# Packing k and v of eight heads so that scores and folds run as eight 64x32 products at a time

## The chip, the cores and the metric

The kernel runs on one core of a Trainium2 chip. The metric is the device time of one execution in microseconds. A core has five engines that run side by side, each through its own list of instructions in order: TensorE (PE in the profile; PEld are its weight loads), VectorE (DVE), ScalarE (ACT), GpSimd (POOL) and SyncE (SP, which here only issues DMAs). TensorE multiplies a stationary matrix, of up to 128 rows and 128 columns here, with a moving one and writes into PSUM, which this kernel uses as eight banks of 512 float32 values on each of 128 partitions. A product may use only some of the array's rows and columns: the profile writes `128*32` for one on all 128 rows and 32 of the columns.

## The reference

```python
def _attn_ref(q, k, v, phi):                 # (8 batches, 8 heads, 576, 64), phi (8, 8, 576, 32)
    a = np.exp(phi - np.max(phi, axis=2, keepdims=True))
    a = a / (np.sum(a, axis=2, keepdims=True) + 1e-09)
    k_m = np.einsum('bhsm,bhsd->bhmd', a, k)          # 32 memories per head
    v_m = np.einsum('bhsm,bhsd->bhmd', a, v)
    scores = (1.0 / np.sqrt(64)) * np.matmul(q, k_m.transpose(0, 1, 3, 2))
    attn = np.exp(scores - np.max(scores, axis=-1, keepdims=True))
    attn = attn / (np.sum(attn, axis=-1, keepdims=True) + 1e-09)
    return np.matmul(attn, v_m)

def _moe_ref(x, w_in, w_out):                # x: (4608, 512), w_in (512, 2048), w_out (2048, 512)
    h = x @ w_in
    return (h * np.cos(h)) @ w_out
```

The attention's output, with the heads side by side, is the x of the second function.

## The kernel before

The product attn · v_m · w_in is regrouped. For each batch `v_m` is multiplied into `w_in` first (the *fold*), which gives a matrix `vw` of 256 rows (8 heads x 32 memories) and 2048 columns, in four quarters `q` of 512 columns. The second layer's input is then attn times `vw`. The 4608 tokens run in 12 groups (`grp`) of 384, and each group in 16 steps `f` of 128 columns of h, 192 steps in all. One step is

- `gemm1` (L493): `hp = vw · aT`, six float16 products, two halves g of the rows times three pairs of high and low parts (12 products of 192 columns in a group that straddles two batches; float32 in group 0),
- `act` and `act_end`: h·cos h by ACT L502, DVE L507 and L508, ACT L512 (the sine), DVE L516 (which is the last to read `hp`), ACT L518 and DVE L519, giving `gp`,
- `gemm2` (L537), four steps behind `gemm1`: nine products that add into three banks `acc`.

The names in the views are those of these tiles: `hp_4_7` is step 7 of group 4, `gp_4_7` what it becomes, `acc_4_0` the first of its sums.

Beside the steps runs the preparation of the next batches, as a generator `prep(b)` that a table of jobs advances a little in each step. `memory(b)` exponentiates phi, multiplies it with k and v in one accumulation `psA` (L247, 40 products), divides by the sums (`X`, L261) and transposes that on TensorE (`tpx`). From `tpx` come `km` and `vm`. `attend(b)` then forms the scores in three blocks of 256, 256 and 64 tokens (L349), transposes each in squares of 32 from PSUM into SBUF on DVE (L351), takes the softmax there and transposes back into `aT`.

Heads lie in pairs: 64 partitions hold an even head's k, the other 64 an odd head's. So `km` is [128, 4 pairs, 64 columns], with the 32 columns of the one head zero on the partitions of the other, and one product of 128 rows and 64 columns makes the scores of two heads. GpSimd clears `km` and `vm` for that in each batch. `vm` is laid out the same way with the halves exchanged, and `fold_psum` uses it for the float32 folds of batch 0 (in `fold_first`, tiles `pvf`) and batch 1. For batches 2 to 7 `scales` splits `vm` into float16 parts: `vp`, the high part on all 128 rows for one head (it meets the high and the low part of `w_in` there), and `vl`, the low part, which has 64 rows of values and 64 of zeros. A fold of half g and quarter q is then four products with `vp` and four with `vl`, all of 128 rows and 32 columns, added in one bank `pv`. `split_fold` turns `pv` into the two float16 parts of `vw` (ACT L438, DVE L439).

PSUM is given out by three pools: `ps_acc` with three banks for `acc`, `ps_h` with three for `hp`, and `ps_s` with two for all small things: the memory products, `tpx`, scores and folds. The order on each engine is set by a scheduler in the framework, which takes the program's order, the pools and its own costs; a wait for a bank or a result holds up everything behind it on that engine.

## Time and profile before

| | |
|---|---|
| median of 3 runs | 718.53 us (717.75 to 719.26) |
| the profiled execution | 718.65 us, of which 716.6 us is the span that the profile shows |
| TensorE busy | 694.8 us, 97% of the span |
| VectorE, ScalarE busy | 570.0 us, 80%, and 520.8 us, 73% |
| GpSimd busy | 14.1 us, 2% |
| gemm2 (L537), gemm1 in float16 (L493) | 1584 and 1440 products |
| folds of batches 2 to 7 (L432) | 384 products |
| scores (L349) | 192 records for 96 products, since a float32 product is two |

Busy times are sums over instructions that may overlap: two products on different columns of the array each count in full. The time between the starts of successive groups in the timeline is the better measure of what something costs on TensorE. An idle engine costs nothing unless the engine at the bound waits for it. In rows by form, the columns are line, engine, operation, output and inputs, the part of the array used, the shape, and the count; then busy time and mean nanoseconds of one; then idle time before, and what ended it.

### The profile page before, as it was taken

The numbers are of one execution on the slowest core, as the hardware profiler recorded it, in microseconds if no ns is written. First come the engines' busy times: TensorE is split into PE (matmuls) and PEld (weight loads), VectorE is DVE, ScalarE is ACT, GpSimd is POOL, SyncE is SP. The second block draws the span as 40 slices with busy tenths as digits, with TensorE's granted clock in tenths as the row PEclk, the third lists the DMA queues.
The fourth block names the chain that finished last, engine by engine and source line by source line (L and its number), as shares of the span: only waits on it lengthen the run. The fifth ranks groups of instructions, "written<-read, shape, count | busy, mean of one in ns | idle before, by whom it ended". The sixth has DMA issues, their size and how long they took to land.

```text
span 716.6 us, 12018 instructions
## 1 busy us (share of the span) xinstructions
PE 694.8 (97%) x4578; PEld 357.2 (50%) x4578; DVE 570.0 (80%) x1256; ACT 520.8 (73%) x965; POOL 14.1 (2%) x34
## 2 busy tenths in 40 slices
PE   7689999999999999999999999999999999999997
PEld 3244444565454445565444544666444544555553
DVE  2868999998988997679877997679776987676753
ACT  1789999899886875668757685678767785665653
POOL 0000000000000000000000100000000000000000
PEclk9799999999999999999999999999999999999999
DMA  8995881426405300152103310152100000100101
GB/s 291 381 330 168 310 291 42 121 60 188 149 7 161 111 1 1 45 167 67 45 1 123 107 49 1 45 167 68 44 1 1 22 24 1 45 1 1 45 0 45
DMA packets 31561, 66.78 MB, mean 93 GB/s; under 512 B 2192, under 2 KB 11024, under 8 KB 31504
## 3 DMA queue, kind: packets, MB, share of 16 engines
q1 hardware_dynamic: 27184, 58.15, 25.1%
q10 hardware_dynamic: 4320, 7.87, 2.9%
q8 instruction: 36, 0.59, 0.3%
q14 instruction: 21, 0.17, 0.1%
HBM read 52.38 MB, written 9.44 MB: 86 GB/s over the span
## 4 chain that ended last, share of the span: by engine, by line
PE 60%; ACT 17%; DVE 16%; DMA 4%; issue 2%; SPq 1%; POOL 0%; ACTq 0%; DVEq 0%
PE acc L537 34%; PE hp L493 18%; PE pv L432 3%; ACT u L512 2%; DVE u L516 2%; DMA phi<-in_phi 2%; DVE u L508 2%; DVE gp L519 2%; ACT u L502 2%; ACT L512 2%; DVE gp L507 1%; DMA kv<-in_kv 1%; PE sc L349 1%; ACT L237 1%; PE psA L247 1%
## 5 line engine op out<-in xcount | busy, mean ns | idle before, releaser
L537 PE MATMUL acc<-wo,gp 128*128 128x512 f16 x1584 | 371.2, 379 | 0.0
L537 PEld LDWEIGHTS <-gp 128*128 128x128 f16 x1584 | 153.4, 98 | 161.5 <-issue 2.6
L493 PE MATMUL hp<-aT,vw 128*128 128x192 f16 (+1 forms) x1440 | 202.6, 284 | 0.8 <-DVE u L516 0.4
L493 PEld LDWEIGHTS <-vw 128*128 128x128 f16 x1440 | 125.1, 98 | 82.3 <-issue 30.0
L512 ACT ACTIVATE u<-u 128x384 f32<-128x384 f32 x192 | 99.7, 522 | 86.6 <-DVE u L508 85.7
L516 DVE SCALAR_TENSOR_TENSOR u<-hp,u 128x384 f32<-128x384 f32 x176 | 96.8, 552 | 45.7 <-ACT u L512 43.4
L502 ACT ACTIVATE u<-hp,cu 128x192 f32<-128x192 f32 (+1 forms) x240 | 110.3, 491 | 18.2 <-PE hp L493 11.8
L519 DVE TENSOR_TENSOR gp<-u,gp 128x384 f16<-128x384 f32 x176 | 96.6, 551 | 29.9 <-ACT gp L518 29.3
L518 ACT CAST gp<-u 128x384 f16<-128x384 f32 x176 | 89.0, 509 | 38.7 <-DVE u L516 36.7
L508 DVE TENSOR_TENSOR u<-u,gp 128x384 f32<-128x384 f32 x192 | 105.7, 552 | 3.2
L507 DVE CAST gp<-u 128x384 int32<-128x384 f32 x192 | 67.4, 353 | 20.6 <-ACT u L502 18.9
L532 PE MATMUL acc<-wo,gp 128*128 128x512 f32 x96 | 45.5, 603 | 1.6 <-DVE gp L514 1.6
L439 DVE SCALAR_TENSOR_TENSOR vw<-pv,vw 128x512 f16<-128x512 f32 x48 | 33.0, 689 | 5.1 <-ACT vw L438 3.8
L438 ACT ACTIVATE vw<-pv 128x512 f16<-128x512 f32 x48 | 28.3, 590 | 7.4 <-PE pv L432 6.5
L484 PE MATMUL hp<-aT,vf 128*128 128x384 f32 x64 | 26.4, 546 | 4.2 <-DVE gp L514 2.0
L512 ACT ACT_TABLE_LOAD x23 | 29.5, 1283 | 0.4
L532 PEld LDWEIGHTS acc<-wo,gp 128*128 128x128 f32 x96 | 17.0, 190 | 20.7 <-issue 14.9
L247 PE MATMUL psA<-kv,phi 128*32 128x129 f32 (+1 forms) x640 | 23.5, 276 | 2.8 <-DMA kv<-in_kv 1.5
L553 ACT ACTIVATE ob<-acc,os 128x512 f32<-128x512 f32 x28 | 18.5, 682 | 8.1 <-PE acc L537 5.2
L247 PEld LDWEIGHTS psA<-kv,phi 128*32 128x32 f32 (+1 forms) x640 | 16.1, 109 | 13.3 <-issue 6.9
L484 PEld LDWEIGHTS hp<-aT,vf 128*128 128x128 f32 x64 | 12.5, 207 | 17.7 <-DVE gp L514 4.6
L349 PE MATMUL sc<-q,km 128*64 128x256 f32 (+3 forms) x192 | 20.6, 343 | 0.0
(126 smaller groups left out, 549.5 us busy)
## 6 DMA issues: line engine op xcount, KB each, us to landing
kv<-in_kv SPq DMA_DIRECT2D x32, 516.0 KB, 5.8
q<-in_qT SPq DMA_DIRECT2D x8, 1152.0 KB, 6.4
raw_out<-in_w_out SPq DMA_DIRECT2D x8, 1024.0 KB, 5.0
out<-ob ACTq DMA_DIRECT2D x30, 256.0 KB, 2.1
raw_in<-in_w_in SPq DMA_DIRECT2D x6, 1024.0 KB, 8.4
phi<-in_phi SPq DMA_DIRECT2D x8, 512.0 KB, 7.2
w_in_sb<-w_in_parts SPq DMA_DIRECT2D x12, 256.0 KB, 4.1
phiT<-in_phiT SPq DMA_DIRECT2D x4, 576.0 KB, 6.4
```

Source lines behind the costliest of these rows:

```text
L247: nc.tensor.matmul(psA[32 * j:32 * (j + 1), g * KV:(g + 1) * KV], lhsT=a[:n, c, h * M:(h + 1) * M], rhs=kvs[c][:n, h * KV:(h + 1) * KV], s ...
L484: nc.tensor.matmul(hp[:, :GT], lhsT=st["vf", q][:, g, fo * P:(fo + 1) * P], rhs=st["aTf"][:, g], start=(g == 0), stop=(g == 1))
L493: nc.tensor.matmul(hp[:, c0:c0 + n], lhsT=vw[:, wi, g, fo * P:(fo + 1) * P], rhs=aT[:, ai, g, c1:c1 + n], start=(k == 0), stop=(k == 5))
L502: ins = nc.scalar.activation(u[:, c0:c0 + n], hp[:, c0:c0 + n], AF.Copy, scale=st["cu", b] if grp else 1.0 / (2.0 * math.pi), bias=0.25)
L507: nc.vector.tensor_copy(out=ni, in_=u)
L508: nc.vector.tensor_tensor(out=u, in0=u, in1=ni, op=ALU.subtract)
L512: nc.scalar.activation(u, u, AF.Sin, scale=TWO_PI_BELOW)
L516: nc.vector.scalar_tensor_tensor(out=u, in0=hp[:, :GT], scalar=2.0 ** -17, in1=u, op0=ALU.mult, op1=ALU.mult)
L518: nc.scalar.copy(gp[:, 0], u)
L519: nc.vector.tensor_tensor(out=gp[:, 1], in0=u, in1=gp[:, 0], op=ALU.subtract)
L532: nc.tensor.matmul(accs[grp][t], lhsT=gp[:, t * P:(t + 1) * P], rhs=wo[:, f + 1], start=(f == 0), stop=(f == NF - 1))
L537: nc.tensor.matmul(accs[grp][t], lhsT=gp[:, gi, t * P:(t + 1) * P], rhs=parts[:, wi], start=(f == 0 and gi == 0 and wi == 0), stop=(f == N ...
```

## The change

Heads 0 to 3 have k on the lower 64 partitions and heads 4 to 7 on the upper; v lies the other way round, and q and `w_in` are laid out on the host to match. So `km`, `vm` and `vl` have no zeros any more and are [128, 4, 32]: row half g belongs to heads 4g to 4g+3, and column j of four to the j-th of these. The clearing of `km` and `vm` on GpSimd, the mask for the maximum of v, and its multiplication on DVE go.

A product with `km`, with float32 `vm`, or with `vl` now uses 64 rows and 32 columns. `scores` and `fold_32` issue eight of them, alternating between the two row halves, and each half writes a bank of its own. A score block so takes two banks of `ps_s` and two transposes in place of one; a fold takes both halves g at once, in one step of four where it was two steps of two. In `fold_16` the first pass with `vp` stays as it was, four products of 128 rows for each g, and the second pass with `vl` is eight products of 64 rows. `fold_first` makes two copies of 256 columns in place of one of 512. To make room in `ps_s`, `psA` is taken from `ps_h`, gemm1's pool.

```diff
-    vl = const.tile([P, NP, 2, M], F16, name="vl")
-    nc.vector.memset(vl, 0.0)
+    vl = const.tile([P, NP, M], F16, name="vl")
...
-        psA = small_ps(f"psA_{b}")
+        psA = ps_h.tile([P, 512], F32, tag="ps_h", name=f"psA_{b}")
...
-        km = wk.tile([P, NP, 2 * M], F32, tag="km", name=f"km_{b}", bufs=1)
-        vm = wk.tile([P, NP, 2 * M], F32, tag="vm", name=f"vm_{b}")
-        nc.gpsimd.memset(km, 0.0)
-        nc.gpsimd.memset(vm, 0.0)
...
+        km = wk.tile([P, NP, M], F32, tag="km", name=f"km_{b}", bufs=1)
+        vm = wk.tile([P, NP, M], F32, tag="vm", name=f"vm_{b}")
+        tv = tpx[:, 0:HM].rearrange("p (g j m) -> p g j m", g=2, m=M)
+        for g in range(2):
+            nc.scalar.mul(km[HALF[g]], tv[HALF[g], g], 1.0 / math.sqrt(D))
+            nc.vector.tensor_copy(out=vm[HALF[1 - g]], in_=tv[HALF[1 - g], g])
...
-        nc.vector.tensor_tensor(out=l1, in0=l1, in1=vmask.rearrange("p g t -> p (g t)"), op=ALU.mult)
...
         def scores(i):
             t0, n = BL[i]
-            sc = small_ps(f"sc_{b}_{t0}")
+            sc = [small_ps(f"sc_{b}_{t0}_{g}") for g in range(2)]
+            for j in range(4):
+                for g in range(2):
+                    nc.tensor.matmul(sc[g][M * j:M * (j + 1), :n], lhsT=km[HALF[g], j], rhs=qt[HALF[g], j, t0:t0 + n],
+                                     start=True, stop=True)
             for g in range(2):
-                for p in range(2):
-                    nc.tensor.matmul(sc[D * p:D * (p + 1), g * n:(g + 1) * n], lhsT=km[:, 2 * g + p],
-                                     rhs=qt[:, 2 * g + p, t0:t0 + n], start=True, stop=True)
-            nc.vector.transpose(at[:, 2 * t0:2 * (t0 + n)], sc[:, :2 * n])
+                nc.vector.transpose(at[:, 2 * t0 + g * n:2 * t0 + (g + 1) * n], sc[g][:, :n])
...
+    def fold_32(b, pv, f):
+        for j in range(4):
+            for g in range(2):
+                v = HALF[1 - g]
+                nc.tensor.matmul(pv[g][M * j:M * (j + 1)], lhsT=st["vm", b][v, j], rhs=w_in_sb[v, j, f],
+                                 start=True, stop=True)
+
+    def fold_16(b, pv, q):
+        w2 = st["w2", q]
+        for g in range(2):
+            for j in range(4):
+                nc.tensor.matmul(pv[g][M * j:M * (j + 1)], lhsT=st["vp", b][:, j, 1 - g], rhs=w2[:, j, 1 - g],
+                                 start=True, stop=False, skip_group_check=True)
+        for j in range(4):
+            for g in range(2):
+                v = HALF[1 - g]
+                nc.tensor.matmul(pv[g][M * j:M * (j + 1)], lhsT=vl[v, j], rhs=w2[v, j, 1 - g],
+                                 start=False, stop=True, skip_group_check=True)
...
-    def fold(b, q, g):
-        if g == 0:
-            st["vw", b, q] = wk.tile([P, 2, 2, FS], F16, tag="vw", name=f"vw_{b}_{q}", bufs=8)
-        split_fold(b, st["vw", b, q], g, fold_psum(b, q, g))
+    def fold(b, q):
+        st["vw", b, q] = vw = wk.tile([P, 2, 2, FS], F16, tag="vw", name=f"vw_{b}_{q}", bufs=8)
+        pv = [small_ps(f"pv_{b}_{q}_{g}") for g in range(2)]
+        if b < 2:
+            fold_32(b, pv, slice(q * FS, (q + 1) * FS))
+        else:
+            fold_16(b, pv, q)
+        for g in range(2):
+            split_fold(b, vw, g, pv[g])
...
-            for g in range(2):
-                folds.setdefault(use - before + 4 * q + 2 * g, []).append((b, q, g))
+            folds.setdefault(use - before + 4 * q, []).append((b, q))
```

What this does to the order of instructions is shown at three places. In these rows each line gives the source line, the operation, output and inputs (with the buffers' numbers) and the shape of the output; line numbers behind the change are shifted by a few.

First, TensorE at the first quarter of batch 4's fold, before:

```order
L537 MATMUL acc_4_2_2937<-wo_85,gp_4_15_3439 128x512
L432 LDWEIGHTS vp_4_3590
L432 MATMUL pv_4_0_0_3598<-w_in_2_0_953,vp_4_3590 32x512
...
L432 LDWEIGHTS vl_86
L432 MATMUL pv_4_0_0_3598<-w_in_2_0_953,vl_86 32x512
...
L493 LDWEIGHTS vw_3_1_2711
```

and after:

```order
L538 MATMUL acc_4_2_3065<-wo_79,gp_4_15_3571 128x512
L427 LDWEIGHTS vp_4_3722
L427 MATMUL pv_4_0_0_3730<-w_in_2_0_1032,vp_4_3722 32x512
...
L427 MATMUL pv_4_0_1_3731<-w_in_2_0_1032,vp_4_3722 32x512
...
L432 LDWEIGHTS vl_80
L432 MATMUL pv_4_0_0_3730<-w_in_2_0_1032,vl_80 32x512
...
L432 MATMUL pv_4_0_1_3731<-w_in_2_0_1032,vl_80 32x512
...
L494 LDWEIGHTS vw_3_1_2828
```

Before, four products with `vp` and four with `vl` stand together for g = 0, and those for g = 1 (pv_4_0_1) two steps later. After, four and four with `vp` for both g are followed by eight with `vl`, which alternate between the two banks.

Second, the scores of batch 5. TensorE before:

```order
L537 MATMUL acc_5_2_3627<-wo_85,gp_5_14_3956 128x512
L349 MATMUL sc_5_0_4156<-q_5_3382,km_5_4073 64x256 x4
L349 MATMUL sc_5_256_4162<-q_5_3382,km_5_4073 64x256 x4
L493 LDWEIGHTS vw_4_0_3597
L493 MATMUL hp_6_3_4168<-aT_4_3259,vw_4_0_3597 128x384
...
L537 MATMUL acc_5_0_3625<-wo_85,gp_5_15_3989 128x512
...
L349 MATMUL sc_5_512_4207<-q_5_3382,km_5_4073 64x64 x4
```

and after:

```order
L538 MATMUL acc_5_2_3770<-wo_79,gp_5_14_4088 128x512
L343 MATMUL sc_5_0_0_4285<-q_5_3514,km_5_4216 32x256
L343 MATMUL sc_5_0_1_4286<-q_5_3514,km_5_4216 32x256
...
L494 LDWEIGHTS vw_4_0_3729
L494 MATMUL hp_6_3_4309<-aT_4_3373,vw_4_0_3729 128x384
...
L343 MATMUL sc_5_256_0_4297<-q_5_3514,km_5_4216 32x256
L343 MATMUL sc_5_256_1_4298<-q_5_3514,km_5_4216 32x256
...
L538 MATMUL acc_5_2_3770<-wo_79,gp_5_15_4121 128x512
...
L343 MATMUL sc_5_512_0_4348<-q_5_3514,km_5_4216 32x64
```

The two blocks of 256 stood next to each other, each in one of the two banks; now each takes both banks, and four products of gemm1 stand between them. On VectorE the same place reads before:

```order
L516 SCALAR_TENSOR_TENSOR u_6_2_4134<-hp_6_2_4127,u_6_2_4134 128x384
L351 STREAM_TRANSPOSE at_5_4153<-sc_5_0_4156 128x512
L519 TENSOR_TENSOR gp_6_2_4135<-u_6_2_4134,gp_6_2_4135 128x384
L351 STREAM_TRANSPOSE at_5_4153<-sc_5_256_4162 128x512
L355 TENSOR_REDUCE rm_5_4154<-at_5_4153 128x16
```

and after:

```order
L517 SCALAR_TENSOR_TENSOR u_6_2_4263<-hp_6_2_4256,u_6_2_4263 128x384
L346 STREAM_TRANSPOSE at_5_4282<-sc_5_0_0_4285 128x256
L346 STREAM_TRANSPOSE at_5_4282<-sc_5_0_1_4286 128x256
L520 TENSOR_TENSOR gp_6_2_4264<-u_6_2_4263,gp_6_2_4264 128x384
L350 TENSOR_REDUCE rm_5_4283<-at_5_4282 128x16
L346 STREAM_TRANSPOSE at_5_4282<-sc_5_256_0_4297 128x256
L346 STREAM_TRANSPOSE at_5_4282<-sc_5_256_1_4298 128x256
```

Each transpose became two of half the size, and the first pair stands ahead of the work that the second block's transposes follow.

Third, TensorE at the memory products of batch 4, with gemm1 of group 4. Before:

```order
L493 MATMUL hp_4_6_3007<-aT_3_2234,vw_3_1_2711 128x192
L537 LDWEIGHTS gp_4_2_2837
...
L493 MATMUL hp_4_7_3059<-aT_3_2234,vw_3_1_2711 128x192
...
L247 MATMUL psA_4_2958<-kv_4_0_2136,phi_4_2133 32x129 x8
L247 MATMUL psA_4_2958<-kv_4_1_2138,phi_4_2133 32x129 x8
...
L537 MATMUL acc_4_2_2937<-wo_85,gp_4_3_2899 128x512
L247 MATMUL psA_4_2958<-kv_4_3_2142,phi_4_2133 32x129 x8
...
L493 MATMUL hp_4_8_3107<-aT_2_1681,vw_2_2_2315 128x192
```

and after:

```order
L538 MATMUL acc_4_2_3065<-wo_79,gp_4_3_3027 128x512
...
L538 MATMUL acc_4_0_3063<-wo_79,gp_4_4_3054 128x512
L245 MATMUL psA_4_3075<-kv_4_0_2249,phi_4_2246 32x129 x8
L494 LDWEIGHTS vw_2_1_2223
L494 MATMUL hp_4_5_3084<-aT_2_1765,vw_2_1_2223 128x192
...
L245 MATMUL psA_4_3075<-kv_4_1_2251,phi_4_2246 32x129 x8
...
L494 MATMUL hp_4_6_3124<-aT_2_1765,vw_2_1_2223 128x192
...
L245 MATMUL psA_4_3075<-kv_4_2_2253,phi_4_2246 32x129 x8
```

Steps 5 and 6 of gemm1, which stood one at a time between the gemm2 products of steps 0, 1 and 2, now stand behind the gemm2 products of steps 0 to 3 and among the memory products. Behind them come the last 16 memory products and four products of gemm2, and then `hp_4_7`, which waits until L517 has read `hp_4_5`.

More of the change, by code (lines that the diff above doesn't have):

```diff
@@ L59, in attention_then_ffn @@
     nc.sync.dma_start(out=ident, in_=eye)
-    vmask = const.tile([P, 2, 2], F32, name="vmask")
-    nc.vector.memset(vmask, 0.0)
-    for j in range(4):
-        nc.vector.memset(vmask[32 * j:32 * (j + 1), :, (j + 1) % 2], 1.0)
+    HALF = (slice(0, D), slice(D, P))
     w_in_sb = const.tile([P, NP, DF], F32, name="w_in_sb")
@@ L450, in fold_first @@
             st["vf", q] = wk.tile([P, 2, FS], F32, tag="vw", name=f"vf_{q}", bufs=8)
[L451 removed]
+        pv = [small_ps(f"pvf_{j}_{g}")[:, 0:WS] for g in range(2)]
+        fold_32(0, pv, slice(j * WS, (j + 1) * WS))
         for g in range(2):
[L453 to L457 removed]
+            (nc.scalar.copy if j < 2 else nc.any.tensor_copy)(out=st["vf", q][:, g, r * WS:(r + 1) * WS], in_=pv[g])
     def split_first(q):
@@ L674, in attention_then_ffn @@
             gemm2(*pending.pop(0))
-        for b, q, g in folds.get(i, ()):
-            if q == g == 0:
+        for b, q in folds.get(i, ()):
+            if q == 0:
                 scales(b)
-            fold(b, q, g)
+            fold(b, q)
         if i % 48 in (8, 24) and i > 8:
@@ L715 @@
     kt, vt = k.transpose(0, 2, 1, 3), v.transpose(0, 2, 1, 3)
[L716 to L717 removed]
+    kv[:, :, :4, 0:D], kv[:, :, :4, D:2 * D] = kt[:, :, :4], vt[:, :, :4]
+    kv[:, :, 4:, 0:D], kv[:, :, 4:, D:2 * D] = vt[:, :, 4:], kt[:, :, 4:]
     laid = {
```

42 lines of the change are left out of this document (7 added, 35 removed).

## The prediction

> **What bounds the kernel now.** I read the page first (engine shares, the slices, the chain of waits), then busy time by stretch, then the timeline of TensorE and VectorE around the folds, the scores and the memory products.
>
> ```profile
> span 716.6 us, 12018 instructions
> PE 694.8 (97%) x4578; PEld 357.2 (50%) x4578; DVE 570.0 (80%) x1256; ACT 520.8 (73%) x965; POOL 14.1 (2%) x34
> ...
> PE   7689999999999999999999999999999999999997
> ...
> PE 60%; ACT 17%; DVE 16%; DMA 4%; issue 2%; SPq 1%; POOL 0%; ACTq 0%; DVEq 0%
> ```
>
> TensorE is busy for 97% of the span and holds 60% of the chain that ended last. The average hides three regimes, which the next view separates: length of the stretch, then busy time of PE, weight load, DVE, ACT and POOL.
>
> ```profile
> core 0: us, PE busy (x) PEld busy (x) DVE busy (x) ACT busy (x) POOL busy (x), PEclk, DMA share, GB/s
> 25.00:110.00 85.00, 78.18 (x334) 36.97 (x335) 74.78 (x152) 81.04 (x119) 1.92 (x6) 0.93 0.81 279
> 110.00:170.00 60.00, 59.67 (x377) 33.07 (x376) 59.53 (x122) 54.97 (x111) 0.31 (x1) 1.00 0.32 80
> 376.00:428.00 52.00, 52.00 (x366) 25.75 (x365) 44.28 (x106) 39.14 (x70) 3.05 (x4) 1.00 0.30 96
> ```
>
> From 25 to 110 us ACT is full (81.04 of 85.00), from 110 to 170 us DVE (59.53 of 60.00); TensorE time saved there buys little. In 376 to 428 us TensorE has no gap and DVE some 15% of slack, and TensorE's slices read 9 from there to the last but one as they do before. So from 170 us on a microsecond saved on TensorE is one off the end, and one in which it waits is one added. The folds of batches 2 to 7 and their scores lie there.
>
> **Folds of batches 2 to 7.** Batch 4's first quarter-fold, half g=1, on TensorE (start, length):
>
> ```profile
> 242.74 1.46 PE L537 MATMUL acc<-wo,gp 128*128 128x512 f16 x6
> 244.03 0.65 PE L493 MATMUL hp<-aT,vw 128*128 128x384 f16 x3
> 244.52 0.81 PE L537 MATMUL acc<-wo,gp 128*128 128x512 f16 x3
> ...
> 245.66 2.11 PE L537 MATMUL acc<-wo,gp 128*128 128x512 f16 x9
> 247.69 0.40 PE L432 MATMUL pv<-w_in_sb,vp 128*32 128x512 f16 x4
> 247.92 0.39 PE L432 MATMUL pv<-w_in_sb,vl 128*32 128x512 f16 x4
> 248.24 1.04 PE L537 MATMUL acc<-wo,gp 128*128 128x512 f16 x4
> ```
>
> Matmuls overlap, so I count from start to start. Six gemm2 products take 244.03 − 242.74 = 1.29, or 0.216 us each; three gemm1 products take 244.52 − 244.03 = 0.49, or 0.163 each; nine gemm2 products end at 245.66 + 1.94 = 247.60. The fold runs from there to 248.24: 0.64 us, made of 0.09 before it, two passes of 0.22, and 0.11 after it. One product of 512 columns takes 0.216 us alone, and here four take no more: the four column strips of the array run fully side by side. The 0.09 and 0.11 are the price of a change of array shape. Per batch and quarter there are two such pieces: 1.28 us.
>
> After the change it is one piece: 0.09, first pass of two groups of four (0.43), a change from 128x32 to 64x32, second pass with eight products, 0.11. The change of shape I price like the two seen, 0.13 at the dearer side. The second pass is not shown by any row: 0.216 us if the two row halves run side by side, 0.43 if they take turns. I take 0.216: the nearest row is the strips, which share fully. So 0.09 + 0.43 + 0.13 + 0.22 + 0.11 = 0.98, a saving of 0.30; 24 pieces give **−7.1 us**; with turns 0.09, so −2.1.
>
> Can TensorE be fed that fast? Sixteen instructions in 0.216 us are 27 ns for a product with its weight load. This row bounds it:
>
> ```profile
> 304.99 1.09 PE L247 MATMUL psA<-kv,phi 128*32 128x129 f32 x32 [0.20 <-ACT phi L237]
> 305.89 0.40 PE L432 MATMUL pv<-w_in_sb,vp 128*32 128x512 f16 x4
> 306.11 0.40 PE L432 MATMUL pv<-w_in_sb,vl 128*32 128x512 f16 x4
> 306.33 0.62 PE L247 MATMUL psA<-kv,phi 128*32 128x129 f32 x16
> 306.88 0.42 PE L493 MATMUL hp<-aT,vw 128*128 128x192 f16 x3
> ```
>
> Thirty-two products, each with its own load, in 0.90 us: 28 ns each. It can, just.
>
> **Scores of batches 2 to 7.** Eight records are four float32 products in two passes.
>
> ```profile
> 232.90 1.08 PE L349 MATMUL sc<-q,km 128*64 128x256 f32 x8
> 233.91 1.15 PE L493 MATMUL hp<-aT,vw 128*128 128x384 f16 x6
> ...
> 190.62 0.45 PE L349 MATMUL sc<-q,km 128*64 128x64 f32 x8
> 191.00 0.60 PE L537 MATMUL acc<-wo,gp 128*128 128x512 f16 x2
> ```
>
> A block of 256 columns takes 1.01 us, one of 64 takes 0.38: 0.63 for 192 columns, so 0.84 and 0.21 for the columns and 0.17 fixed. Products two at a time become eight at a time but twice as many, so the column part halves: −0.42 and −0.105. Per batch 2 × 0.42 + 0.105 = 0.945; six batches **−5.7 us** (0 with turns).
>
> **The wait that this brings.** Each score block now takes both banks of the pool `ps_s`, and two transposes must empty both before the next block or fold starts. Batch 4's scores, batch 5's and batch 7's, and when DVE got to them:
>
> ```profile
> 320.33 1.08 PE L349 MATMUL sc<-q,km 128*64 128x256 f32 x8
> 402.27 1.95 PE L349 MATMUL sc<-q,km 128*64 128x256 f32 x16
> 404.15 1.15 PE L493 MATMUL hp<-aT,vw 128*128 128x384 f16 x6
> 563.40 1.95 PE L349 MATMUL sc<-q,km 128*64 128x256 f32 x16
> ```
> ```profile
> 324.04 0.72 DVE L351 STREAM_TRANSPOSE at<-sc 128x512 f32<-128x512 f32 x1
> 405.25 0.70 DVE L351 STREAM_TRANSPOSE at<-sc 128x512 f32<-128x512 f32 x1
> 406.38 0.71 DVE L351 STREAM_TRANSPOSE at<-sc 128x512 f32<-128x512 f32 x1
> 564.81 0.70 DVE L351 STREAM_TRANSPOSE at<-sc 128x512 f32<-128x512 f32 x1
> ```
> ```profile
> L372 DVE STREAM_TRANSPOSE aT<-at 128x256 f32<-128x256 f32 x2 | 0.8, 424 | 0.0
> ```
>
> Two transposes of 256 columns take 0.85 us instead of one of 0.71. In batch 5 the two blocks stand four gemm1 products apart in the new order: 4 × 0.163 = 0.65 us of cover. DVE came 1.9 us after the first block's end (402.27 + 1.08 = 403.35 to 405.25): 1.9 + 0.85 − 0.65 = 2.1 us of waiting. Batch 7's delay was 564.81 − 564.48 = 0.3: 0.5, and I take 1.0 with its third block. Batches 2, 4 and 6 have a whole step, 1.0 + 1.94 us, between blocks: batch 4's delay of 2.6 (to 324.04) + 0.85 exceeds that by 0.5. Batch 2 none. Batch 3's third block is split around the gemm1 products that follow its second, which covers 0.65 of a delay that I take as batch 7's 0.3 plus 0.85, and once more 0.6 for its second half: 1.1. Sum 1.1 + 0.5 + 2.0 + 0.5 + 1.0 = **+5.1 us**; 0 if DVE comes at once, 8 if each of these is half as long again.
>
> The Trainium skill, *TensorEngine Tiling (Array Packing)*, "Gotcha 1: PSUM Pressure", speaks against the change in the same way: row tiles write different PSUM banks, may not share one at a time, and software has to synchronise. No row here shows two row tiles; by that rule alone the sum would keep this term, and without it stand 5.1 us lower.
>
> **The memory products in gemm1's pool.** `psA` now holds one of three `ps_h` banks from its first product until DVE has read it, so gemm1 waits for the bank of two steps back instead of three. That bank is free when DVE's multiplication L516 has read it. A short and a long case, while the products of batch 5 and of batch 4 run:
>
> ```profile
> 384.57 1.15 PE L493 MATMUL hp<-aT,vw 128*128 128x384 f16 x6
> 387.98 0.56 DVE L516 SCALAR_TENSOR_TENSOR u<-hp,u 128x384 f32<-128x384 f32 x1
> ```
> ```profile
> 311.45 0.56 DVE L516 SCALAR_TENSOR_TENSOR u<-hp,u 128x384 f32<-128x384 f32 x1
> ```
>
> From gemm1's end to L516's end: 388.54 − 385.72 = 2.8 us, and 312.01 − 307.30 = 4.7 (its gemm1 ends with the row at 306.88). In the new order hp_4_7 waits for hp_4_5's bank, and between stand 32 psA products (0.90), hp_4_6 (1.0), four gemm2 products (0.86) and three changes of shape: 3.1 us. So nothing to 1.6 us of waiting, once in each of six batches: 0 to 9.5. I take 0.5 each, **+3 us**, nearer the short case: four steps of gemm2 products (4 × 1.94 = 7.8 us) now stand between hp_4_4 and hp_4_5, in which ACT and DVE can work off what is queued.
>
> **Edits that I cost at nothing.**
>
> ```profile
> L457 ACT COPY vf<-pvf 128x512 f32<-128x512 f32 x5 | 2.9, 576 | 2.9 <-PE pvf L455 2.9
> L457 DVE COPY vf<-pvf 128x512 f32<-128x512 f32 x3 | 2.1, 684 | 0.0
> L426 PE MATMUL pv<-w_in_sb,vm 128*64 128x512 f32 x32 | 9.7, 618 | 0.0
> L283 DVE TENSOR_TENSOR l<-l,vmask 128x4 f32<-128x4 f32 x8 | 1.3, 158 | 0.2
> ```
>
> Start-up: the 8 copies of 512 columns become 16 of 256; at 424 ns on DVE some 1.3 us more there, with batch 0's and 1's transposes 0.9 more, 0.3 less for the masks of those batches. DVE is not the bound there. ACT, the bound to 110 us, gets eight copies of half the size for five. Four loads of an activation table fall away behind 160 us, where ACT is not the bound. Batch 1's float32 fold takes half the column time, some 4.5 us of TensorE inside DVE's stretch, where it hides. Net 0, between −4.5 (if TensorE does bound there) and +3. The removed memsets and zero halves lie on POOL, idle for 98%.
>
> **Sum** against the profiled run, 718.65 (the median is 718.53): −7.1 − 5.7 + 5.1 + 3 + 0 = −4.7, so **714 us**. Under 0.2%, 1.4 us, counts as no change.
>
> **Rivals.** (1) Neither wait comes, since DVE reaches transposes and releases as early as batch 7's 0.3 us: 718.65 − 12.8 = 705.9. Against it, batch 5's 1.9. (2) The eight overlap only in part: midway between the two ends the second pass takes 0.32, folds give 24 × 0.195 = 4.7 and scores 2.85: 718.65 − 7.5 + 8.1 = 719.2. For it only that no row shows row halves; against it, the strips. The Trainium skill, *TensorE: Matmul & The Clock Gate*, Part 3, "Measured speedup vs the span model", gives 6.32 times for nine tiles and 10.6 for sixteen, two thirds of the count; by that eight give an estimated 5.6 and the time comes out close to this case. The trace does not agree for four, which here give the full four (0.216). (3) The change doesn't do what it says: the two row halves take turns. −2.1 for folds, 0 for scores, +3.5 of waits (longer blocks cover more), +3: 723. (4) gemm1 starves while psA holds its bank: at the long case 9.5, with the transposes' waits at 8: −12.8 + 17.5 = +4.7, 723.3. It decides for slower once both waits together pass 12.8, 2.1 us a batch. For it: DVE at 85% in the stretch of batch 5's work, so that a queue is there to be late; against it: the gemm2 steps that let it drain.
>
> **Chances.** Forecast 0.50 (own range 708 to 718); (1) 0.10; (2) 0.10; (3) 0.11; (4) 0.19. Range of all 705 to 724, which leaves the far tails out. Faster: the forecast but for its upper tail (0.46), (1), and 0.05 of the others' lower tails: 0.61. Same: 0.03 of the forecast and most of (2): 0.12. Slower: the rest, 0.27, mostly (3) and (4).
>
> **What would show it.** Folds: second-pass start to next start 0.22 + 0.11, a piece of 0.98 instead of two of 0.64. Scores: 0.6 us a block. Waits: gaps on TensorE before batch 5's and 7's second block, released by the transposes, and before the second gemm1 step after each psA's start, released by L516. Wrong if the second pass takes 0.4, or if those gaps add up to over 13 us.

## The result, and the profile after

The changed kernel takes 729.46 us (728.17 to 730.30, four runs) against 718.89 (717.75 to 720.32) for the kernel before: the ratio is 1.0144, with an interval of 1.012 to 1.0169, so it is slower by 1.4%. The forecast was 714.0, in a range of 705 to 724. The execution profiled takes 729.79 us with a span of 728.0, 11.4 more than before's 716.6.

The page of the changed kernel, its span, engines, TensorE's 40 slices, and the shares of the chain that ended last:

```profile
span 728.0 us, 12569 instructions
PE 686.6 (94%) x4866; PEld 348.5 (48%) x4866; DVE 570.6 (78%) x1272; ACT 512.9 (70%) x963; POOL 8.6 (1%) x18
...
PE   7589889989999999999999999999999999999997
...
PE 44%; DVE 31%; ACT 14%; DMA 7%; issue 2%; SPq 1%; ACTq 0%; POOL 0%; DVEq 0%; POOLq 0%
```

TensorE is busy 8.2 us less, and its share of the chain falls from 60% to 44% while DVE's rises from 16% to 31%. The work shrank, and waits, for DVE above all, took its place. The three stretches shown before, now:

```profile
core 0: us, PE busy (x) PEld busy (x) DVE busy (x) ACT busy (x) POOL busy (x), PEclk, DMA share, GB/s
25.00:110.00 85.00, 72.23 (x427) 30.77 (x428) 74.92 (x156) 81.23 (x119) 0.70 (x2) 0.92 0.81 275
110.00:170.00 60.00, 55.75 (x378) 31.97 (x377) 57.45 (x119) 52.18 (x109) 0.58 (x1) 1.00 0.29 76
376.00:428.00 52.00, 50.78 (x391) 24.17 (x390) 41.47 (x100) 35.24 (x65) 1.79 (x2) 1.00 0.30 96
```

In the last stretch TensorE, without a gap before, now has 1.22 us of them. Those gaps over the whole steady part are named by the list of what TensorE waits for from 190 us on (line, what it waited for: us in total, times, longest), first of the kernel before:

```profile
PE pv L432 <- ACT vp L317: 0.4, 1, 0.4
PE psA L247 <- ACT phi L237: 0.4, 2, 0.2
PE hp L493 <- DVE u L516: 0.3, 1, 0.3
```

and of the changed one:

```profile
PE acc L538 <- ACT ob L554: 2.7, 6, 0.9
PE hp L494 <- DVE u L517: 2.4, 4, 1.0
PE sc L343 <- DVE at L346: 2.2, 3, 1.0
PE sc L343 <- DVE vm L271: 1.3, 2, 0.7
PE tpx L265 <- DVE vw L438: 1.1, 1, 1.1
PE tpx L265 <- DVE X L259: 0.6, 2, 0.4
...
```

1.1 us became 11. Two lines were forecast (`hp` waits for `u`, `sc` for `at`). Three kinds were not: `sc`, which waits until the copies to `vm` (L271) have emptied the bank of `tpx`; `tpx`, which once waits for a bank of the small pool until `vw` (L438) has emptied it; and `acc`, gemm2's own bank, which waits for the copy `ob` (ACT, L554) that empties it at the end of a group.

What the prediction priced on TensorE itself came out. The fold of batch 4's first quarter, start and length:

```profile
246.83 2.11 PE L538 MATMUL acc<-wo,gp 128*128 128x512 f16 x9
248.87 0.61 PE L427 MATMUL pv<-w_in_sb,vp 128*32 128x512 f16 x8
249.41 0.41 PE L432 MATMUL pv<-w_in_sb,vl 64*32 64x512 f16 x8
249.75 0.50 PE L494 MATMUL hp<-aT,vw 128*128 128x384 f16 x2
```

Nine gemm2 products end at 246.83 + 1.94 = 248.77, so the piece takes 249.75 − 248.77 = 0.98 us, as forecast. Its second pass takes 249.75 − 249.41 = 0.34; if 0.11 of that is the change of shape at its end, as it was before the change, 0.23 are left for eight products of 512 columns, where one alone takes 0.216. Batch 4's scores:

```profile
333.16 0.66 PE L343 MATMUL sc<-q,km 64*32 64x256 f32 x16
333.75 1.16 PE L494 MATMUL hp<-aT,vw 128*128 128x192 f16 x12
...
336.79 0.34 PE L343 MATMUL sc<-q,km 64*32 64x64 f32 x16
337.07 1.16 PE L494 MATMUL hp<-aT,vw 128*128 128x192 f16 x12
```

0.59 us for a block of 256 columns and 0.28 for one of 64, again the forecast's 1.01 − 0.42 and 0.38 − 0.105.

**Where the 11.4 us are.** The first gemm2 product of group 2 stands at 184.54 us before and 5.2 us later behind the change; the rest of the span is longer by 6.1. I split that rest by what stands on TensorE: from the start of one kind of work to the start of the next, less 0.163, 0.083 or 0.216 us for each product of gemm1 and gemm2. So a wait counts with the work that it delays (in us; "start" is the delay against before at that gemm2 product; the names of the variants are explained below). Each row is the one execution that was profiled, up to 2.6 us away from the median of its kernel, and another rule for the gaps between two kinds of work would move single entries by up to 0.6:

| profiled run | start | folds | scores | psA | tpx | gemm1 waits | gemm2 waits | rest in all |
|---|---|---|---|---|---|---|---|---|
| before | 0 | 31.4 | 14.2 | 15.1 | 2.3 | 1.3 | −0.2 | 532.1 |
| after | +5.2 | 25.4 | 15.9 | 16.3 | 5.2 | 4.1 | 3.5 | 538.2 |
| psA as before | +3.9 | 27.3 | 19.1 | 15.0 | 2.2 | 1.6 | 4.6 | 537.7 |
| scores in one bank | +3.9 | 26.0 | 14.1 | 16.7 | 4.3 | 4.0 | 3.6 | 536.5 |
| both (folds only, e4) | +0.1 | 27.3 | 16.2 | 15.9 | 3.2 | 0.3 | 3.7 | 534.5 |
| folds by halves (e5) | −1.7 | 36.5 | 14.0 | 15.1 | 2.6 | 1.1 | −0.2 | 537.0 |
| folds only, old start (e9) | −0.4 | 28.0 | 16.8 | 15.8 | 2.9 | −0.1 | 3.4 | 534.7 |
| e9, psA in `ps_h` (e10) | −1.5 | 25.8 | 14.1 | 16.7 | 3.9 | 3.9 | 3.4 | 535.7 |
| e10, second split later (e22) | −1.6 | 26.5 | 19.2 | 16.0 | 2.9 | 3.4 | 0.6 | 536.4 |

After against before, by the unrounded figures: folds −6.1, scores +1.7, psA +1.1, tpx +2.9, gemm1 +2.8, gemm2 +3.8, and the start +5.2. How far two starts differ by themselves can be seen in e16 below: it does the same work in the same order as the kernel before up to 290 us, and is 1.9 us earlier from 50 us on. So a start within 2 us of before's counts as on time. The experiments ask which part of the change each of these belongs to.

### The profile page after: what moved, and what is told of

Read it like the earlier page. It is cut to its first block, busy times and chain, and to the rows that moved or that the text cites. A ratio compares the mean times of both kernels' runs of the same rounds, so it can differ in the third digit from the quotient of the medians.

```text
span 728.0 us, 12569 instructions
## 1 busy us (share of the span) xinstructions
PE 686.6 (94%) x4866; PEld 348.5 (48%) x4866; DVE 570.6 (78%) x1272; ACT 512.9 (70%) x963; POOL 8.6 (1%) x18
## 4 chain that ended last, share of the span: by engine, by line
PE 44%; DVE 31%; ACT 14%; DMA 7%; issue 2%; SPq 1%; ACTq 0%; POOL 0%; DVEq 0%; POOLq 0%
PE acc L538 26%; PE hp L494 12%; DVE u L509 5%; DVE u L517 5%; DVE gp L520 4%; ACT u L513 3%; DVE gp L508 3%; DMA phi<-in_phi 2%; DVE vw L438 2%; DMA raw_out<-in_w_out 2%; ACT u L503 2%; ACT gp L519 1%; DMA kv<-in_kv 1%; DVE w_in_parts L187 1%; PE pv L427 1%
## 5 line engine op out<-in xcount | busy, mean ns | idle before, releaser
L517 DVE SCALAR_TENSOR_TENSOR u<-hp,u 128x384 f32<-128x384 f32 x176 | 96.8, 553 | 45.1 <-ACT u L513 42.5
L438 DVE SCALAR_TENSOR_TENSOR vw<-pv,vw 128x512 f16<-128x512 f32 x48 | 31.1, 684 | 2.8 <-ACT vw L437 2.7
L533 PEld LDWEIGHTS acc<-wo,gp 128*128 128x128 f32 x96 | 17.5, 192 | 20.6 <-issue 14.4
L437 ACT ACTIVATE vw<-pv 128x512 f16<-128x512 f32 x48 | 26.0, 589 | 0.4 <-PE pv L432 0.2
L554 ACT ACTIVATE ob<-acc,os 128x512 f32<-128x512 f32 x28 | 18.6, 683 | 8.5 <-PE acc L538 6.1
L343 PE MATMUL sc<-q,km 64*32 64x256 f32 (+3 forms) x384 | 18.5, 334 | 5.1 <-DVE at L346 2.8
L245 PEld LDWEIGHTS psA<-kv,phi 128*32 128x32 f32 (+1 forms) x640 | 15.9, 108 | 14.1 <-issue 8.0
L485 PEld LDWEIGHTS hp<-aT,vf 128*128 128x128 f32 x64 | 12.2, 207 | 19.2 <-issue 7.1
```

The costliest lines, as they stand in the source:

```text
L245: nc.tensor.matmul(psA[32 * j:32 * (j + 1), g * KV:(g + 1) * KV], lhsT=a[:n, c, h * M:(h + 1) * M], rhs=kvs[c][:n, h * KV:(h + 1) * KV], s ...
L438: nc.vector.scalar_tensor_tensor(out=vw[:, 1, g], in0=src, scalar=T, in1=vw[:, 0, g], op0=ALU.mult, op1=ALU.subtract)
L517: nc.vector.scalar_tensor_tensor(out=u, in0=hp[:, :GT], scalar=2.0 ** -17, in1=u, op0=ALU.mult, op1=ALU.mult)
L533: nc.tensor.matmul(accs[grp][t], lhsT=gp[:, t * P:(t + 1) * P], rhs=wo[:, f + 1], start=(f == 0), stop=(f == NF - 1))
```

## Experiments: one part taken back

Two theories stood ahead of these: that `psA` in gemm1's pool makes the loss (A), or that scores and folds need both small banks at once (B).

**The memory products in the small pool again.**

```diff
-        psA = ps_h.tile([P, 512], F32, tag="ps_h", name=f"psA_{b}")
+        psA = small_ps(f"psA_{b}")
```

> The changed kernel with one line back: psA of every batch is taken from ps_s again, all else as changed. Theory A (gemm1's pool): the time was lost because psA holds one of gemm1's three banks; then the gaps of about 4 us before gemm1 behind 190 us and the 5 us lost before group 2 go, and the time is 720 to 722 us, with scores and folds as fast as in the changed kernel. Theory B (two banks): the time was lost because scores and folds need both banks of ps_s at once; then psA makes that worse, since no score block or fold can start while it holds one of the two: 730 to 740 us, with gaps before folds and scores.

730.31 us, ratio 1.0163 (1.0105 to 1.022): no better, as B has it, though the four runs lie as far apart as 726.6 and 734.6 and the one in the table took 727.88. What moved there: gemm1's waits fall from 4.1 to 1.6 and psA's time from 16.3 to 15.0, but scores rise from 15.9 to 19.1 and folds by 2.0, now that a third user competes for the two small banks.

For batches 0 and 1 alone the same edit (`small_ps(...) if b < 2 else ps_h.tile(...)`):

> The changed kernel with psA of batches 0 and 1 alone taken from ps_s again; from batch 2 on it stays in gemm1's pool. If the 5.2 us that were lost before group 2 come from psA_1 pushing gemm1's steps 3 and 4 of group 0 back, the start-up returns to before: 724 to 725 us and group 2's gemm2 starts at 184.5 instead of 189.7. If they come from the float32 folds' and scores' pairs of banks there, nothing is won: 728 to 731 us.

729.96 us, 1.015 (1.011 to 1.019). Start-up is 4.9 us late instead of 5.2: psA's place in the first two batches is not, by itself, what delays it.

**Scores in one bank**, `km` padded with zeros, one transpose:

```diff
-            sc = [small_ps(f"sc_{b}_{t0}_{g}") for g in range(2)]
+            sc = small_ps(f"sc_{b}_{t0}")
...
+                    nc.tensor.matmul(sc[M * j:M * (j + 1), g * n:(g + 1) * n], lhsT=km[:, j, g],
+                                     rhs=qt[:, j, t0:t0 + n], start=True, stop=True)
+            nc.vector.transpose(at[:, 2 * t0:2 * (t0 + n)], sc[:, :2 * n])
```

> The changed kernel with the scores alone taken back: km has zero halves again (cleared on GpSimd), a score block is eight products of 128 rows and 32 columns, four at a time, into one bank, with one transpose. Folds and psA stay as changed. Theory A: the 4 us of scores saved are lost and only some 4 us of waits before scores come back: 728 to 731 us. Theory B: with one bank a block also the folds and tpx find a free bank sooner, start-up included: 722 to 726 us.

727.30 us, 1.0127 (1.0087 to 1.0166), between the two ranges. Scores return to 14.1 us, before's 14.2, so in the changed kernel the cheaper score blocks lose 1.7 us net to their waits. gemm1 and gemm2 wait as they did.

**Folds of batches 1 to 7 by halves**, one bank and two steps apart as before, the second pass four products of 64 rows:

```diff
-            folds.setdefault(use - before + 4 * q, []).append((b, q))
+            for g in range(2):
+                folds.setdefault(use - before + 4 * q + 2 * g, []).append((b, q, g))
```

> The changed kernel with the folds of batches 1 to 7 alone taken back to one half g at a time, in steps of two, one bank each; the second pass is then four products of 64 rows on one row half. Scores (two banks) and psA stay as changed. If the eight-wide second pass and the fewer changes of shape are worth what the sum says, 24 x 0.2 to 0.3 us are lost: 734 to 737 us. If folds with two banks at once bring waits of their own as large as that, 727 to 730 us.

740.97 us, 1.0291 (1.0244 to 1.0337): the slowest, beyond both ranges. The folds take 37.4 us, 12 more than in pairs; scores rise too, to 19, and the start is 7.6 us late. A pass of four products of 64 rows takes as long as one of 128 did, and each of the 48 pieces has one more change of array shape. In the variant e5 below, where nothing else competes for banks, 48 pieces take 36.5 instead of 31.4: 0.11 us for that change. gemm2's waits fall to 1.9 here, and its list of waits has none for `ob` any more: the first hint that this wait belongs to the pair.

**psA and scores as before, all folds as changed:**

> The changed kernel with two things back for all batches: psA in ps_s and the scores in one bank. The float32 folds of batches 0 and 1 and the float16 folds keep both halves at once in two banks. Taking back either alone left 3.9 us of loss at group 2's first gemm2, taking back everything in batches 0 and 1 left none. If two causes stand side by side in the start (psA in gemm1's pool, score blocks in two banks), the start is now that of before, within 1 us, and the time 719 to 721 us; if the float32 folds in two banks are a third cause, 2 to 4 us of loss stay there: 722 to 725 us.

721.66 us, 1.0035 (1.0019 to 1.005). Together they return 7.8 us, where alone psA returned nothing (−0.9) and the scores 2.2. Most of it is the start: +5.2 with both, +3.9 with either one, +0.1 with none. So start-up needs both parts taken back, and either suffices to delay it; the float32 folds in two banks, still in this kernel, cost it nothing that can be seen.

## Experiments: the start

Batches 0 and 1 wholly as before, all else as changed:

```diff
+        psA = small_ps(f"psA_{b}") if b < 2 else ps_h.tile([P, 512], F32, tag="ps_h", name=f"psA_{b}")
...
+            if b < 2:
+                sc = small_ps(f"sc_{b}_{t0}")
...
+            for gs in ((0,), (1,)) if b < 2 else ((0, 1),):
+                folds.setdefault(use - before + 4 * q + 2 * gs[0], []).append((b, q, gs))
```

> The changed kernel with batches 0 and 1 treated as before the change: km and vm with zero halves, scores in one bank with one transpose a block, fold_first in one bank with one copy, batch 1's folds by halves, psA in ps_s. Batches 2 to 7 as changed. The runs so far lose 3.9 to 7.6 us before group 2's first gemm2, whichever single part is taken back. If the two-bank float32 folds and scores of the start cause that, it goes: 184.5 us there and 723 to 725 us in all. If any other order of the start costs as much (it is bound by ScalarE and VectorE in turn), 3 to 6 us stay: 728 to 731 us.

723.66 us, 1.0065 (1.0043 to 1.0086). Start-up is on time (−0.6), and the rest is as late as in the changed kernel (537.7). About half of the loss is thus start-up, by edits to two batches that the forecast costed at nothing.

How they act there is seen in part, on ACT, which is busy for 81.23 of the 85 us from 25 to 110 us. It loads an activation table ahead of batch 1's exponentials and another ahead of the next sine of a step, and no step's sine runs between the two loads. This happens twice, at 48 us for `phi` and at 74 us for the scores. Before:

```profile
48.09 1.28 ACT L237 ACT_TABLE_LOAD   x1
...
51.18 1.28 ACT L512 ACT_TABLE_LOAD   x1
...
74.38 1.28 ACT L405 ACT_TABLE_LOAD   x1
...
82.62 1.28 ACT L512 ACT_TABLE_LOAD   x1
```

After:

```profile
48.16 1.28 ACT L235 ACT_TABLE_LOAD   x1
...
57.97 1.28 ACT L513 ACT_TABLE_LOAD   x1
...
78.14 1.28 ACT L400 ACT_TABLE_LOAD   x1
...
87.40 1.28 ACT L513 ACT_TABLE_LOAD   x1
```

3.1 us became 9.8, and 8.2 became 9.3. With `psA` alone in gemm1's pool (e2) the first stretch is 10.1 us, with scores alone in two banks (e1, e6) it is 3.1 again, but behind it come two stretches, of 5.3 and 9.0. Up to 100 us the stretches without a sine sum to 17.4 to 19.1 us in all six profiles that start late, and to 10.7 to 11.3 in all the others. So each of the two edits lengthens a stretch of its own, and the late starts have 6 to 8 us more of them (the sum is 17.4 with either edit, 19.1 with both). This is a pattern across the profiles: no run changes the stretches alone, and why the order on ACT came out so stays open.

## Experiments: the folds alone

**All as before except the layout of the heads and the float16 folds of batches 2 to 7 in pairs** (e8's start; one-bank scores; psA in `ps_s`):

> Batches 0 and 1 as before the change, scores in one bank and psA in ps_s for all batches; of the change only the float16 folds of batches 2 to 7 stay, both halves at once in two banks with the eight-wide second pass. By the folds' price alone (24 x 0.2 to 0.3 us saved, start as before) 711 to 714 us. If a fold that needs both banks waits for psA, scores or split_fold to leave them, the saving is eaten: 718 to 722 us, with gaps before the folds of 2 us and more.

720.48 us, 1.0019 (1.0007 to 1.0031). **The same with psA of batches 2 to 7 in `ps_h`:**

> As the kernel before it in this job, but psA of batches 2 to 7 in gemm1's pool ps_h. The difference between the two is the price of psA's place: if the banks of gemm1 cost, this one is 3 to 5 us slower (gaps before gemm1 in six batches); if psA in the way of the folds costs more, it is 2 to 5 us faster.

722.66 us, 1.0038 (1.0021 to 1.0056). This is 2.2 us more, not the 3 to 5 of the first case. Folds save 3.4 and 5.6 us, and neither kernel is faster than before. What they save returns as waits. TensorE's waits from 190 us on, e9:

```profile
PE acc L544 <- ACT ob L560: 2.6, 6, 0.9
PE sc L350 <- ACT km L277: 2.2, 4, 0.6
...
```

and e10:

```profile
PE acc L544 <- ACT ob L560: 2.7, 6, 0.9
PE hp L500 <- DVE u L523: 2.5, 2, 1.2
...
```

psA's place moves a wait from one pool to the other: in `ps_s` scores pay 2.7 us and folds 2.2, in `ps_h` gemm1 pays 4.0, `tpx` 1.0 and psA 0.9. gemm2's wait is in both.

**Folds by halves with the 64-row second pass, psA and scores as before** (in `fold_first` two banks stay):

> The changed layout, but scores in one bank, psA in ps_s, and the folds of batches 1 to 7 by halves with a four-wide second pass; only the float32 folds of batch 0 (fold_first) still take two banks with two copies, and vm and vl have no zero halves. Nothing is saved and nothing waits for two banks behind the start: if fold_first alone loses the 4 to 5 us of the start, 722 to 724 us; if the start is as before here, 718 to 720 us.

722.58 us, 1.005 (1.0028 to 1.0072). The time lies in the range that I gave for a late start, but for another reason: the start, with `fold_first` in two banks, is on time (−1.7), and the folds are 5.1 us dearer. gemm2 does not wait (−0.2, as before). So gemm2's 3.5 us come with taking both halves at once.

**Why the pair makes gemm2 wait.** ACT's timeline in the changed kernel, where group 3's sums end and group 4's begin:

```profile
297.35 0.51 ACT L519 CAST gp<-u 128x384 f16<-128x384 f32 x1 [0.62 <-DVE u L517]
...
299.57 0.52 ACT L513 ACTIVATE u<-u 128x384 f32<-128x384 f32 x1 [1.08 <-DVE u L509]
300.72 0.51 ACT L519 CAST gp<-u 128x384 f16<-128x384 f32 x1 [0.62 <-DVE u L517]
301.14 1.08 ACT L437 ACTIVATE vw<-pv 128x512 f16<-128x512 f32 x2
302.10 0.69 ACT L554 ACTIVATE ob<-acc,os 128x512 f32<-128x512 f32 x1
```

In this step ACT idles twice, 1.08 us for DVE ahead of the sine and 0.62 ahead of the cast `gp`. A single fold copy into `vw` takes 0.58 (a row of it follows below). One fits into such a gap. A pair, 1.08 us in a row, does not, and what stands behind it is late; here `ob`, for which gemm2's next sum waits:

```profile
302.85 0.81 PE L538 MATMUL acc<-wo,gp 128*128 128x512 f16 x3 [0.38 <-ACT ob L554]
...
304.00 2.32 PE L538 MATMUL acc<-wo,gp 128*128 128x512 f16 x10 [0.35 <-ACT ob L554]
```

e10 with the second half's copies put two steps later, in a fixed order, tests that:

```diff
-        for g in gs:
-            split_fold(b, vw, g, pv[g])
+        split_fold(b, vw, gs[0], pv[gs[0]])
+        for g in gs[1:]:
+            late.append((step[0] + 2, (b, vw, g, pv[g])))
```

> The kernel of e10_folds_only_psA_h (folds of both halves at once, psA in gemm1's pool, scores in one bank, start as before) with the second half's copies to vw two steps after the first half's, its bank held so long. If the pair of copies on ScalarE makes gemm2 wait for the emptying of acc, the waits at the start of groups 4 and 7 go (some 2 us less): 718 to 720 us against some 722 us, with gemm1's waits for L516 left as they are. If the waits stay, the same 721 to 723 us; slower, 724 us and more, if the bank that is held longer stops scores or tpx.

723.76 us, 1.0052 (1.0033 to 1.007), not the 718 to 720 of the first case. ACT's copies now stand apart and in the gaps:

```profile
292.17 0.52 ACT L522 ACTIVATE u<-u 128x384 f32<-128x384 f32 x1 [1.23 <-DVE u L518]
292.60 0.58 ACT L442 ACTIVATE vw<-pv 128x512 f16<-128x512 f32 x1
293.32 0.51 ACT L528 CAST gp<-u 128x384 f16<-128x384 f32 x1
293.74 0.68 ACT L563 ACTIVATE ob<-acc,os 128x512 f32<-128x512 f32 x1
```

and of TensorE's waits the one for `ob` is almost gone, with another in its place:

```profile
PE sc L350 <- DVE vw L445: 3.7, 3, 1.5
PE hp L503 <- DVE u L526: 1.5, 4, 0.6
...
PE acc L547 <- ACT ob L563: 0.4, 1, 0.4
```

gemm2's share falls from 3.4 to 0.6: that the copies stand two in a row is what held `ob` up in e10. It is not the only way to this wait, as e11 shows below. Scores rise from 14.1 to 19.2, since the second half holds its bank two steps longer: the wait moved, and grew.

## Experiments: can the folds' gain be kept?

Later folds for odd batches (two steps) on e9, then on e10, and for all batches from 3 on e9:

```diff
-                folds.setdefault(use - before + 4 * q + 2 * gs[0], []).append((b, q, gs))
+                folds.setdefault(use - before + 4 * q + 2 * gs[0] + (2 if b > 2 and b % 2 else 0), []).append((b, q, gs))
```

> The kernel of e9_folds_only (start as before, scores in one bank, psA in ps_s, float16 folds of both halves at once) with the folds of batches 3, 5 and 7 two steps later, so that their pairs of copies to vw on ScalarE stand behind and not in front of the copies that empty acc at the end of groups 3, 6 and 9. If that pair of copies is what makes gemm2 wait 3.3 us at the start of groups 4, 7 and 10, these waits fall under 0.5 us and the time is 717 to 718 us; if the wait has another cause, 720 to 721 us as before the shift.

> The kernel of e10_folds_only_psA_h (psA of batches 2 to 7 in gemm1's pool) with the same shift of the folds of batches 3, 5 and 7 by two steps. The waits of gemm2 should go as in the other; the waits of gemm1 for L517, some 3 us, should stay: 718 to 720 us. If the shift also clears gemm1's waits, 715 to 717 us.

> As e11_folds_later, with the folds of batches 4 and 6 two steps later too. If only the folds ahead of a group's end matter, the same time as e11 within 1 us; if folds in general stand in the way of psA and scores in ps_s, 2 us less or more.

721.06 (1.0023, 1.0006 to 1.004), 719.64 (1.0017, 1.0004 to 1.003) and 721.74 us (1.0047, 1.003 to 1.0064). gemm2's waits stay at 3.1, 3.1 and 4.8: by what I had written ahead of e11, they had another cause than the pair. e11's rows at the same place, the end of group 3:

```profile
295.75 0.51 ACT L525 CAST gp<-u 128x384 f16<-128x384 f32 x1 [0.62 <-DVE u L523]
296.17 0.68 ACT L560 ACTIVATE ob<-acc,os 128x512 f32<-128x512 f32 x1
```
```profile
296.90 0.81 PE L544 MATMUL acc<-wo,gp 128*128 128x512 f16 x3 [0.99 <-ACT ob L560]
```

No pair stands ahead of `ob` now, and gemm2 waits 0.99 us for it instead of 0.35. With the fold gone from the last steps of the group, TensorE is there some 0.98 us sooner, the time of one fold, while ACT still has to wait for DVE ahead of its cast. So the pair explains the wait that e22 takes away; behind it stands, as I read these rows, that TensorE gets ahead of the steps on ACT and DVE where it has no other work. e12 is the best of the variants that keep the paired folds, and still not faster than before.

`ob` of three groups on DVE instead of ACT, on e12 and on the kernel before:

```diff
-        elif grp == 11 and t == 1:
+        elif grp == 11 and t == 1 or grp in (3, 6, 9) and t == 0:
```

> The kernel of e12_folds_later_psA_h with the copy that empties the first acc bank of groups 3, 6 and 9 on VectorE instead of ScalarE. If gemm2 waits at the start of groups 4, 7 and 10 because that copy stands in ScalarE's queue behind a cast that waits for VectorE, the first of the two waits there (some 0.4 to 1 us each) goes and the second shrinks: 1.5 to 3 us less, 717 to 718 us. If the wait moves to VectorE's queue, the same 719 to 720 us.

> The kernel before the change with the same copies on VectorE. It has no wait of gemm2 there, so nothing is to be won: 718 to 719 us by the theory that the wait comes with the folds of both halves; 716 to 717 us if the copy's engine matters by itself.

723.27 us, 1.005 (1.0036 to 1.0064), and 718.27 against 720.04, 0.9976 (0.9966 to 0.9987). On e12 the wait went into DVE's queue (`acc` then waits 2.1 us for `ob` on DVE and 1.6 on ACT), and the time is 3.6 us worse than e12's. On the kernel before, 1.9 us of the profiled gain already stand before group 0's step 4, where the edit has no instruction and the order of work is the same: two executions differ by that much. Behind the start the trace gains 0.5 us, so why the median is 1.8 us lower stays open.

Two steps in flight on ACT and DVE from group 2 on and not only from group 9 (`act_end` one step behind `act`), on e12, before and after:

```diff
-        while len(begun) > (grp >= 9):
+        while len(begun) > (grp >= 2):
```

> The kernel of e12_folds_later_psA_h (folds of both halves, scores in one bank, start as before) with act_end one step behind act from group 2 on instead of from group 9 on, so that two steps are in flight on ScalarE and VectorE. If the hand-overs of one step at a time end last, the waits of gemm2 and gemm1 shrink by 3 us or more: 714 to 717 us. If not, 719 to 721 us; slower, 722 us and more, if gemm1's banks are then held longer, since L516 reads hp one step later.

> The kernel before the change with the same edit. It has next to no waits, so by the theory little is to be won: 717 to 719 us; slower if gemm1's banks are held longer, 720 to 724 us.

> The changed kernel as it is with the same edit. By the theory some 3 us of its 7 us of waits of gemm1 and gemm2 go and the start's 5 us stay: 724 to 727 us; if banks of gemm1 are held longer while psA has one of them, 730 to 736 us.

721.21 (1.0024, 1.0006 to 1.0042), 717.56 (0.9979, 0.9962 to 0.9996) and 731.97 us (1.0165, 1.0139 to 1.0191); the last is the dearer of its two cases. It does not help where banks are short: in e17 folds sink to some 24 us and scores to 13.0, while psA and `tpx` rise to some 19 and 6.2. On the kernel before it gains 2.5 us behind group 2's first gemm2 product and loses 1.7 ahead of it. e16 and e18, edits to the kernel before without anything of the change, are the only versions faster than both kernels, each by 0.2%.

## The prediction, step by step

- **A fold piece of 0.98 us, 24 of them for −7.1.** Right for the piece, 0.98; −6.1 in all, waits included. (Two roundings are 0.1 off: 24 × 0.30 is 7.2, and batch 5's wait, worked out as 2.1, stands as 2.0 in its sum. They change nothing.)
- **Eight 64x32 products side by side.** Right: 0.23 us against 0.216 for one. So rivals 2 (partial overlap) and 3 (turns) fall. The estimate of 5.6 times (0.70 of the count, as for nine tiles) from the Trainium skill, *TensorE: Matmul & The Clock Gate*, Part 3, "Measured speedup vs the span model", would make it 8 × 0.216 / 5.6 = 0.31; the trace gives 8 × 0.216 / 0.23, or 7.5 times.
- **Scores: −5.7 by products, +5.1 by waits.** Each block's price was right. At 0.59 and 0.28 six batches would take 8.8 us; they take 15.9, so 7.1 go to waits and to blocks that are split or start late. The mechanism was right, its size short by 2.0: I had priced the second transpose but not the bank that `vm`'s two copies out of `tpx` hold (`sc` waits for `vm`, 1.3 us), nor that `tpx` itself comes to wait (+2.9, of which the list of waits shows 1.1 for a bank that a fold held and 0.6 for its input `X`). This is the pressure that the Trainium skill's *TensorEngine Tiling (Array Packing)*, "Gotcha 1: PSUM Pressure", warns of, and the trace agrees, with two more users of the pool than I counted.
- **psA in gemm1's pool, +3.** gemm1 +2.8 and psA +1.1: right within 1 us. That the small pool costs about as much (by e9 and e10, 4.9 us there against 5.9) was not asked.
- **"Start-up … Net 0", −4.5 to +3.** Wrong, +5.2, outside the bounds given. I priced copies, transposes and saved products one by one and set them against the engine that was full, and looked past two things: that psA takes a gemm1 bank also in batches 0 and 1, and that their score blocks hold both small banks, on engines that had no slack. Either one alone costs 3.9. The loads of activation tables I had counted only behind 160 us, where four fall away; ahead of 100 us the stretches between them grew by 6 to 8 us.
- **No term for gemm2.** I named the queue behind DVE's transposes, and for the pair of fold copies on ACT only the total, which does not change. That they come two in a row does, and gemm2's waits grow by 3.8 us.
- **The sum.** With what was measured for each term: −6.1 + 1.7 + 2.9 + 2.8 + 1.1 + 3.8 + 5.2 = +11.4, where the forecast had −4.7. The terms that I had priced (folds, scores, `psA` and gemm1) come to −6.1 + 1.7 + 1.1 + 2.8 = −0.5, which alone would be hardly any change. So the step that failed is the list of who waits: the start stood in it at nothing, and `tpx` and gemm2 not at all, and these three cost 5.2 + 2.9 + 3.8 = 11.9 us. Rivals 3 and 4 came nearest with 723 and 723.3, but not by their mechanisms: 3 falls by the 0.23 us, and 4 has the two waits that I had named decide for slower past 12.8 us, where they came to 7.1 + 3.9 = 11.0. Neither of the two signs that I had given for being wrong appeared: the second pass took 0.23 us and not 0.4, and the named gaps came to 2.2 + 2.4 us and not to 13. Both signs looked only at terms of the sum.

The deeper fault was to take "TensorE has no gap here" for "a microsecond saved is one off the end". Even e9 and e10, which have only the saving on folds, don't end earlier. Two small banks and ACT's and DVE's chain of one step stood just behind TensorE. At the change from group 3 to group 4 that chain takes 3.37 us a step (300.72 − 297.35, cast to cast), where gemm1 and gemm2 take 1.0 + 1.94 = 2.94 on TensorE. The kernel before has the same 3.37 there:

```profile
285.84 0.51 ACT L518 CAST gp<-u 128x384 f16<-128x384 f32 x1
...
289.21 0.51 ACT L518 CAST gp<-u 128x384 f16<-128x384 f32 x1 [0.62 <-DVE u L516]
```
```profile
284.98 1.16 PE L493 MATMUL hp<-aT,vw 128*128 128x192 f16 x12
...
291.50 1.16 PE L493 MATMUL hp<-aT,vw 128*128 128x192 f16 x12
```

Its TensorE, with half a fold in every second step, takes (291.50 − 284.98) / 2 = 3.26: in these steps it was no slower than the chain even then, in which ACT and DVE wait for each other alone, and time saved on TensorE there runs into the chain. That this holds for the whole steady part is argued from such steps, not shown by a run. e17 and e18, in which two steps overlap, gain 0.5 and 2.5 us behind the start.

## What to carry to other kernels

Count for how long a packed product holds its banks, and who else draws on that pool, as carefully as its time on the array: here 6 us saved on folds cost 17.5 in waits and in start-up (the other terms of the sum above). Before a saving on the busiest engine is counted, the next longest chain of the same step is to be measured: here 3.37 us against 3.26. A copy that fits into an engine's idle gap costs nothing alone and delays what is behind it when two come in a row, so a fusion that keeps the number of copies can still cost. Give the part of the program with another bound than the rest its own forecast, and there price waits too, not instructions alone.

## What the runs showed of the hardware

Two row halves of the array worked fully side by side here, where each wrote a bank of its own (no run has both in one bank): eight float16 products of 64 rows and 32 columns take 0.23 us where one takes 0.216. A change from 128x32 to 64x32 within a fold costs about 0.11 us (5.1 us over 48 pieces in e5), about as much as the changes from and to 128x128. So halving the rows paid only where both halves ran: by halves it made the folds 5.1 us dearer. A load of an activation table took 1.28 us, but its price here was the stretch in which no sine ran, 3.1 to 10.1 us for the same exponentials.
